# Placing the inverse exit of the second chunk pair by hand between the hidden-layer products of chunk 1

## The chip, the cores and the metric

The kernel runs on one core of a Trainium2 chip. The metric is device time in microseconds (us), from launch to end; the median of five runs of the kernel before is 590.45 us (586.62 to 592.89). Five engines work side by side, each through its own instructions in order: PE (TensorE, matrix products, with its weight loads shown as PEld), DVE (VectorE), ACT (ScalarE), POOL (GpSimd) and SP (SyncE, which only issues DMAs here). An instruction that waits for another engine holds up everything behind it on its own engine.

## The reference, cut to what matters

```python
# attention: delta rule, B=4, H=8, S=768, D=48
k_n = k / (norm(k) + 1e-6)
state = zeros(B, H, D, D)
for t in range(S):
    y[t]  = q[t] @ state                       # the state before this step's update
    v_old = state^T k_n[t]
    state = state + beta[t] * outer(k_n[t], v[t] - v_old)
# bridge (B,H,S,D) -> (B,S,384), then the MLP block
xn  = (x - mean(x)) / sqrt(var(x) + 1e-6) * g_ln
out = x + relu(xn @ w_ch1) @ w_ch2             # 384 -> 1536 -> 384
```

All of it is in float32.

## The kernel before, in words

The sequence is cut into 12 chunks of 64 tokens, and the 32 heads (batch times head) are laid out so that two batches share the 128 partitions. Within a chunk the recurrence is solved in closed form: the Gram matrix of the keys (`p_g`, line 358) is turned into the inverse of a unit triangular matrix (`xt`), and with it `recur` computes, in steps named KQ (products with the state, `p_k` and `p_y`, L640, then `v_raw` minus `p_k` on DVE, L645), U (L651), S (state update, L663 and L666), PU (L671), L1 and L2 (layer norm statistics) and N (transposes, L698). Chunks go in pairs.

**The inverse.** `inverse` works on DVE in a layout in which every partition holds one small block: a loop over columns, two instructions per column (L543, L548). For the first two pairs (`first_blocks`) the blocks are 16 by 16. The way out is `scatter`: two masked copies into `x_e` (L496) and a transpose into `own` (L499) for each chunk. From there `first_join` puts the 16-blocks together to blocks of 32: a transpose `x_n` (L593), 64 small matmuls `p_e` (L598), a copy with the sign changed on ACT (`es`, L601), 64 small matmuls `p_z` (L606) and an addition into `own` on DVE (L607). `to_xt` writes the blocks into `xt` (DVE L451 and ACT L453). `join` does the same once more, from 32 to 64, with `x_n` L559, `p_e` L568, `es` L581, `p_z` L614 and copies L619 on DVE and ACT. Its products for the second chunk of a pair are interleaved with the `p_z` of the first.

**The MLP.** `hidden` computes the 12 row blocks of the hidden layer of a chunk (`p_h`, L732, three matmuls each; `h` by ACT L736). Chunk 0 uses `ffn` (L749, sums on DVE L757); later chunks use `mlp`, with seven half-size products P1 to P7 (L787) and sums S1 to S4 and d1 to d7 on DVE (L792). It needs differences of blocks of the second weight matrix, made once (`sum_blocks`, L716, token T).

**What sets the order.** The first stretch (chunk 0 up to its layer norm) is written out in order. The second stretch is a `Plan`: generators are spread over a time axis by due times, and a scheduler orders the result; it holds chunk 1's recurrence, the hidden and output products of chunk 0, the weights and the preparation of chunks 2 and 3, among it the whole of the second pair's inverse and its joins. From chunk 2 on, each chunk is a slot whose order is a string of tokens, taken in exactly that order on every engine. The slots are not tied behind the plan, so the scheduler places the last instructions of the plan among the first of slot 2. In slot 2, H is one row block of chunk 1's hidden layer, KQ, U, S, PU, L1, L2 and N are steps of chunk 2's recurrence, T one block of `sum_blocks`, TK, TQ, G and PT prepare chunks 3 to 5, ga, sq and no begin the inverse of the next pair, Vk and Vs scale the next values by the key norms (`norms`, L402 to L410; `scale_v`, L418).

PSUM tiles are shared by tags: `p_o` of `ffn` and `p_h` take the same two buffers, and `p_e`, `p_z` and `p_n` take the same two.

Of the kernel before, what the change touches and what calls it, by code (L numbers as in the profile page):

```python
# [19 lines left out]
FB = 16  # L20
SLAB = 2
# [55 lines left out]
def in_turn(*gens):  # L77
    for gen in gens:
        yield from gen
# [3 lines left out]
def kernel(  # L83
# [23 lines left out]
    B, H, S, D = q.shape  # L107
    NCH = S // C
    NSL = NCH // SLAB
# [17 lines left out]
    def ps_att(shape, name):  # L127
        return psum.tile(shape, FP32, name=name, tag="att", bufs=2)
# [263 lines left out]
    def swapped(name):  # L392
        return blk.tile([128, 2 * FB * FB], FP32, name=name, tag="tr", bufs=2)

    def norm_parts(c, scratch=None):

        parts = [
            scratch[:, n::2, 0:D] if scratch is not None
            else swapped("ksq")[:, 0 : H * D].rearrange("p (h d) -> p h d", d=D)
            for n in range(2)  # L400
        ]
        nc.scalar.square(parts[0], k_of(c)[:, 0::2])  # L402
        for e in range(2):
            nc.scalar.square(parts[1][half(e)], k_of(c)[half(1 - e), 1::2])
        yield
        ksum = work.tile([128, GH], FP32, name="ksum")
        for n in range(2):
            nc.vector.tensor_reduce(out=ksum[:, n::2], in_=parts[n], axis=mybir.AxisListType.X, op=ALU.add)
        knrm = work.tile([128, GH], FP32, name="knrm")
        nc.scalar.sqrt(knrm, ksum)  # L410
        yield knrm

    def norms(c):
        *_, knrm = norm_parts(c)
        return knrm

    def scale_v(c, knrm):
        nc.vector.scalar_tensor_tensor(  # L418
            out=vs[c], in0=knrm[:, :, None].to_broadcast([128, GH, D]), scalar=1e-6, in1=vs[c],
            op0=ALU.add, op1=ALU.mult,  # L420
        )
# [7 lines left out]
    def prep_g(c, fine=False):  # L429

        new_chunk(c)
        turned(c, 0, True)
        yield
        for _ in gram(c, fine):
            pass
        yield

    def prep_p(c):

        turned(c, 1, True)  # L440
        yield
        yield from product(c)
        yield
# [4 lines left out]
    def to_xt(c, eng=None):  # L448

        xt, own = xts[c % NXT], halves.pop(c)  # L450
        nc.vector.tensor_scalar(out=xt[:, :, 0:BK], in0=own, scalar1=is_u[:, 0:1], scalar2=None, op0=ALU.mult)  # L451
        if eng is None:
            nc.scalar.copy(xt[:, :, BK:C], own)  # L453
        else:
            eng.tensor_copy(out=xt[:, :, BK:C], in_=own)
# [19 lines left out]
    def first_blocks(chunks):  # L475

        def gather(gb):
            for n, c in enumerate(chunks):
                tr = swapped("g_t").rearrange("p (s t) -> p s t", t=BK)
                nc.vector.transpose(  # L480
                    tr.rearrange("p s (b h) -> p s b h", b=2),
                    grams[c][:, :, 0:BK].rearrange("p h (b s) -> p s b h", b=2),
                )
                nc.vector.tensor_scalar(
                    out=gb[:, n], in0=tr[:, :, 0:FB], scalar1=is_b[:, 0:1], scalar2=None, op0=ALU.mult
                )
                nc.vector.scalar_tensor_tensor(
                    out=gb[:, n], in0=tr[:, :, FB:], scalar=is_b[:, 1:2], in1=gb[:, n], op0=ALU.mult, op1=ALU.add
                )

        def scatter(xb):
            own = blk.tile([128, len(chunks), GH, BK], FP32, name="own", tag="gb")
            for n, c in enumerate(chunks):
                xe = swapped("x_e").rearrange("p (b s t) -> p b s t", b=2, t=FB)
                for b in range(2):
                    nc.vector.tensor_scalar(  # L496
                        out=xe[:, b], in0=xb[:, n], scalar1=is_b[:, b : b + 1], scalar2=None, op0=ALU.mult
                    )
                nc.vector.transpose(  # L499
                    own[:, n].rearrange("p h (b t) -> p t b h", b=2), xe.rearrange("p b s t -> p t b s")  # L500
                )
                halves[c] = own[:, n]
                yield

        c0 = chunks[0]
        return inverse(len(chunks), FB, beta_f[:, c0 : c0 + len(chunks)], gather, scatter)
# [82 lines left out]
    def first_join(c):  # L589

        own, gsb = halves[c], grams[c]
        xn = swapped("x_n").rearrange("p (h t) -> p h t", t=BK)
        nc.vector.transpose(xn, own)  # L593
        quarters = [slice(BK * n, BK * n + BK) for n in range(4)]
        p_e = ps_att([128, GH, FB], "p_e")
        for h in range(GH):
            for q in quarters:
                nc.tensor.matmul(p_e[q, h], gsb[q, h, 0:BK], xn[q, h, 0:FB])  # L598
        es = work.tile([128, GH, BK], FP32, name="es", bufs=1)
        nc.gpsimd.memset(es[:, :, FB:], 0.0)  # L600
        nc.scalar.mul(es[:, :, 0:FB], p_e, -1.0)  # L601
        yield
        p_z = ps_att([128, GH, FB], "p_z")
        for h in range(GH):
            for q in quarters:
                nc.tensor.matmul(p_z[q, h], es[q, h], own[q, h, FB:])  # L606
        nc.vector.tensor_tensor(out=own[:, :, FB:], in0=own[:, :, FB:], in1=p_z, op=ALU.add)  # L607
        yield
# [326 lines left out]
    plan = Plan()  # L935
# [9 lines left out]
    plan.spread(ffn_0, FT // 2, 20, 42)  # L945
    plan.once(10, queries)
    plan.spread(in_turn(*(prep_g(c, True) for c in (2, 3))), 4, 16, 24)
    plan.spread(first_blocks((2, 3)), 5 + FB // 2, 24, 44)
    plan.spread(prep_p(2), 2, 30, 38)

    def then(c):
        yield from first_join(c)
        to_xt(c)
        yield

    plan.spread(in_turn(then(2), then(3)), 6, 44, 56)
    plan.once(50, lambda: scale_v(2, norms(2)))
    plan.spread(join((2, 3)), 4, 56, 62)
    with behind(tc, after):
        plan.run()  # L960

# [2 lines left out]


    orders = {
        2: """KQ H H H H H H T H T H T H T H U H H TK(a2) P1 S1 S2 d1 TK(b2) S P2 d2 S4 PU P6 d6
            S3 L1 G(a2) P5 d5 L2 TQ(b) P7 d7 N G(b2) P3 d3 ga PT(b) P4 d4 sq no Vk
            Vs""",
        3: """KQ H r H r H r H r U TQ(a2) H r H r H r S H r H r H H H PU P1 L1 S1 S2 d1 PT(a2) P2  # L970
            d2 L2 S4 P6 d6 S3 TK(a4) P5 d5 r N r P7 d7 G(a4) TK(b4) P3 d3 r G(b4) P4
            d4 r Vk Vs""",
# [13 lines left out]
    def slot(c, order):  # L986

        a = c - c % SLAB
        names = {"b": a + 1, "a2": a + 2, "b2": a + 3, "a4": a + 4, "b4": a + 5}
        begin(c)  # L990
        steps = mlp(c - 1)
        chunk = recur(c)
        if c + 2 < NCH:
            load_kv(c + 2)
        knrm = None
        for token in order.split():
            name, _, arg = token.partition("(")
            m = c // SLAB + (name[-1] != "'")
            name = name.rstrip("'")
            x = names[arg[:-1]] if arg else None  # L1000
            if name in steps:
                steps[name]()
            elif name in ("KQ", "U", "S", "PU", "L1", "L2", "N"):
                if not (name == "S" and c == NCH - 1):
                    next(chunk)
            elif name == "T":
                next(running_sums)
            elif name == "R":
                for _ in range(left.get(m, 0)):
                    next(inverses[m])  # L1010
                left[m] = 0
            elif name in ("ga", "sq", "no", "r", "own", "xt"):
                if m in inverses:
                    left[m] -= name == "r"
                    next(inverses[m])
            elif name in ("xn", "J"):
                if m in joins:
                    next(joins[m])
            elif name == "Vk":
                if c + 1 < NCH:  # L1020
                    knrm = norms(c + 1)
            elif name == "Vs":
                if c + 1 < NCH:
                    scale_v(c + 1, knrm)
            elif x < NCH:
                if name == "TK":
                    new_chunk(x)
                    turned(x, 0, True)
                elif name == "TQ":
                    turned(x, 1, True)  # L1030
                elif name == "G":
                    next(gram(x), None)
                elif name == "PT":
                    for _ in product(x):
                        pass

    running_sums = sum_blocks()
    inverses = {m: blocks(m) for m in range(2, NSL)}
    joins = {m: join((SLAB * m, SLAB * m + 1)) for m in inverses}
    left = {m: BK // 2 - 1 for m in inverses}  # L1040
    with in_this_order(tc):
        for c in range(SLAB, NCH):
# [34 lines left out]
```

## Time and profile before

| what | value |
| --- | --- |
| median of five runs | 590.45 us (586.62 to 592.89) |
| time of the profiled execution | 589.51 us |
| its span, first to last instruction | 587.4 us |
| mean granted TensorE clock | 0.948 |
| PE busy | 536.5 us (91%), 9938 matmul records |
| DVE busy | 384.3 us (65%) |
| ACT busy | 173.3 us (30%) |
| `p_h` L732 | 864 records, 202.5 us |
| `p_e`, `p_z` of the first joins, L598 and L606 | 512 records each, over four chunks |

A float32 matmul stands in the records twice, each with its own weight load; so one H is 6 records, one product of `first_join` is 128, of `join` 64, and KQ is 64 for `p_k` and 64 for `p_y`. The profile cuts the span into 40 slices and shows for each the busy share of every engine and the granted clock in tenths. In the timeline, "idle before" is time in which the engine did nothing, with what released it; "issue" there means that it waited for nothing that the profile shows.

### The profile page before, as it was taken

What the parts mean: (1) busy time and instruction counts of PE and PEld (TensorE: products, weight loads), DVE (VectorE), ACT (ScalarE), POOL (GpSimd) and SP (SyncE); (2) the same over time, 40 slices, a digit from 0 to 9 for tenths busy, and PEclk for the clock granted to TensorE, in tenths of its full rate; (3) what the DMA queues carried; (4) which work ended last, traced back from release to release, by engine and by line L of the source; (5) the groups of instructions that cost most, each with busy time, mean ns of one, the idle gap of its engine ahead of it and who ended that gap; (6) DMA issues with size and microseconds to landing.
All of it is one profiled execution on the core that took longest, in us unless ns stands there. A gap on an engine that the chain in (4) does not pass through costs nothing.

```text
span 587.4 us, 21790 instructions
## 1 busy us (share of the span) xinstructions
PE 536.5 (91%) x9938; PEld 459.2 (78%) x9938; DVE 384.3 (65%) x795; ACT 173.3 (30%) x355; POOL 16.3 (3%) x39
## 2 busy tenths in 40 slices
PE   5389886966999999999979999999999999999997
PEld 2165664655889898789878899888898898998997
DVE  5857978875236998489993889764899731522312
ACT  1233353111325215422216312336312142223120
POOL 5000200000000000000000000000000000000000
PEclk9568988885899999999999999999999999999999
DMA  4745979452123505222233313303303010010101
GB/s 57 142 156 115 216 173 204 74 89 41 20 26 59 88 7 83 57 30 50 42 48 61 63 19 66 45 4 68 46 8 77 2 30 2 2 29 1 28 0 28
DMA packets 158667, 34.57 MB, mean 59 GB/s; under 512 B 153952, under 2 KB 157040, under 8 KB 158576
## 3 DMA queue, kind: packets, MB, share of 16 engines
q1 hardware_dynamic: 144048, 22.28, 23.3%
q0 software_dynamic: 1456, 7.10, 3.8%
q10 hardware_dynamic: 13072, 3.80, 2.8%
q8 instruction: 78, 1.28, 0.9%
q14 instruction: 13, 0.11, 0.1%
HBM read 28.44 MB, written 4.72 MB: 56 GB/s over the span
## 4 chain that ended last, share of the span: by engine, by line
PE 70%; DVE 10%; issue 9%; ACT 3%; DMA 3%; SPq 1%; ACTq 1%; POOL 0%; DVEq 0%; POOLq 0%
PE p_h L732 30%; PE p_a L787 12%; PE p_o L787 9%; PE p_g L358 2%; DVE tmp L543 2%; DVE xb L548 2%; DMA words<-in_moe_w_ch_dram 2%; PE p_u L651 2%; PE p_e L568 2%; PE p_y L640 2%; PE p_y L671 2%; PE p_s L663 2%; PE p_k L640 2%; PE p_g L383 2%; PE p_z L614 2%
## 5 line engine op out<-in xcount | busy, mean ns | idle before, releaser
L732 PE MATMUL p_h<-xnt,w_sb 128*128 128x256 f32 x864 | 202.5, 390 | 0.7 <-ACT xnt L699 0.6
L732 PEld LDWEIGHTS p_h<-xnt,w_sb 128*128 128x128 f32 x864 | 163.8, 193 | 25.1 <-ACT xnt L699 0.9
L736 ACT ACTIVATE h<-p_h 128x256 f32<-128x256 f32 x144 | 55.2, 383 | 143.3 <-PE p_h L732 136.5
L548 DVE TENSOR_TENSOR xb<-xb,tmp 128x31 f32<-128x31 f32 (+20 forms) x154 | 50.1, 326 | 5.3
L787 PE MATMUL p_a<-t,h 128*128 128x192 f32 x264 | 47.1, 328 | 1.0 <-DVE h L792 1.0
L787 PE MATMUL p_o<-w_sb,h 128*128 128x192 f32 x264 | 48.0, 332 | 0.0
L543 DVE TENSOR_TENSOR tmp<-xb,gb 128x31 f32<-128x31 f32 (+15 forms) x124 | 42.0, 339 | 3.2
L787 PEld LDWEIGHTS p_a<-t,h 128*128 128x128 f32 x264 | 42.8, 190 | 1.5 <-DVE h L792 1.2
L787 PEld LDWEIGHTS p_o<-w_sb,h 128*128 128x128 f32 x264 | 42.7, 190 | 0.9
L682 DVE BATCH_NORM_STATS2 st<-x_ln 128x6 f32<-128x384 f32 x24 | 12.9, 542 | 34.9 <-ACT x_ln L676 34.8
L830 PE MATMUL p_w<-zeros 128*64 128x512 f32 (+1 forms) x30 | 20.1, 809 | 14.0 <-DVE zeros L827 10.8
L619 DVE COPY xt<-p_z 32x512 f32<-32x512 f32 x12 | 8.1, 679 | 29.6 <-PE p_z L614 29.6
L792 DVE TENSOR_TENSOR s<-h 128x768 f32<-128x768 f32 x11 | 10.2, 931 | 26.4 <-ACT h L736 26.4
L787 PE MATMUL p_a<-t,s 128*128 128x192 f32 x132 | 23.6, 329 | 2.9 <-DVE o L792 2.8
L699 ACT COPY xnt<-p_n 128x384 f32<-128x384 f32 x24 | 10.3, 482 | 48.9 <-PE p_n L698 48.8
L787 PEld LDWEIGHTS p_a<-t,s 128*128 128x128 f32 x132 | 21.5, 190 | 3.9 <-DVE o L792 3.7
L787 PE MATMUL p_a<-w_sb,h 128*128 128x192 f32 x132 | 24.2, 333 | 0.0
L787 PE MATMUL p_o<-w_sb,s 128*128 128x192 f32 x132 | 23.6, 328 | 0.0
L358 PEld LDWEIGHTS p_g<-kt 48*32 48x32 f32 (+1 forms) x1024 | 14.1, 125 | 11.4 <-issue 8.3
L358 PE MATMUL p_g<-kt 48*64 48x64 f32 (+2 forms) x1024 | 16.0, 225 | 6.8 <-issue 5.3
L830 PEld LDWEIGHTS p_w<-zeros 128*64 128x64 f32 x30 | 4.8, 184 | 21.8 <-DVE zeros L827 10.9
L787 PEld LDWEIGHTS p_a<-w_sb,h 128*128 128x128 f32 x132 | 21.3, 190 | 0.6
(123 smaller groups left out, 728.8 us busy)
## 6 DMA issues: line engine op xcount, KB each, us to landing
words<-in_moe_w_ch_dram POOLq DMA_DIRECT2D x9, 768.0 KB, 5.8
out_dram<-o SPq DMA_DIRECT2D x48, 96.0 KB, 3.3
k<-in_k_dram SPq DMA_DIRECT2D x44, 96.0 KB, 2.8
v_raw<-in_v_dram SPq DMA_DIRECT2D x22, 192.0 KB, 4.1
tb<-in_k_dram SPq DMA_DIRECT2D x48, 64.0 KB, 2.8
tb<-in_q_dram SPq DMA_DIRECT2D x44, 64.0 KB
words<-in_moe_w_ch_dram ACTq DMA_DIRECT2D x3, 768.0 KB
tb<-in_q_dram SPq DMA_DIRECT2D x44, 32.0 KB, 2.2
```

Of the source, the lines that this page charges most:

```text
L358: nc.tensor.matmul(out_, kt[rows, i, r0 : r0 + (BK if fine else C)], kt[rows, i, r0:C])
L383: nc.tensor.matmul(p_g[half(e ^ hp), hp, j], kt[rows, i], qt[rows, i])
L543: nc.vector.tensor_tensor(out=t, in0=xb[:, :, 0:n, j : j + 1].to_broadcast([128, nb, n, w]), in1=gb[:, :, j : j + 1, j + 1 : L].to_broadca ...
L548: nc.vector.tensor_tensor(out=rest, in0=rest, in1=t, op=ALU.subtract)
L568: nc.tensor.matmul(p_e[r1, h], gsb[r0, h, BK:C], xn[r0, h])
L614: nc.tensor.matmul(p_z[r0, h], es[r1, h], xt[r1, h, BK:C])
L640: nc.tensor.matmul(dst[half(e), hp, j], kq[n][rows, e * GP + j], s_all[rows, e, j], start=(n == 0 or j == 0), stop=(n == 0), skip_group_ch ...
L682: nc.vector.bn_stats(out=st[:, g], in_=y[:, g])
L732: nc.tensor.matmul(p_h, w1_sb[:, t, f * 128 : (f + 1) * 128], xnt[:, t], start=(t == 0), stop=(t == KC - 1),)
L736: nc.scalar.activation(h[f // HF][:, f % HF], p_h, ACTF.Relu)
L787: nc.tensor.matmul(p[n], a[:, f], b[:, f], start=(first and f == 0), stop=(f == HF - 1), skip_group_check=True,)
L830: nc.tensor.matmul(p_w[0:64, 0:width], zeros, zeros[:, None, :].to_broadcast([128, width, 64]), start=True, stop=True,)
```

## The change

The steps that bring the second pair (chunks 2 and 3) out of the block layout leave the plan and become tokens in slot 2. The column loop stays in the plan; its spread ends at due time 42 in place of 44 and is not run to its end. X is one step of `scatter` (one chunk), F one half of `first_join`, W `to_xt`, J' one step of `join` of this pair. The squares, sums and scaling for chunk 2's values (`norms` and `scale_v`) move from due time 50 to 28. Within slot 2, S and PU now stand ahead of P1, and U, T, TK(a2), TK(b2), L1, L2 and N have other places. No arithmetic is added or left out.

```diff
-    plan.spread(first_blocks((2, 3)), 5 + FB // 2, 24, 44)
+    inv_1 = first_blocks((2, 3))
+    plan.spread(inv_1, 2 + FB // 2, 24, 42, whole=False)
     plan.spread(prep_p(2), 2, 30, 38)
-    def then(c):
-        yield from first_join(c)
-        to_xt(c)
-        yield
-    plan.spread(in_turn(then(2), then(3)), 6, 44, 56)
-    plan.once(50, lambda: scale_v(2, norms(2)))
-    plan.spread(join((2, 3)), 4, 56, 62)
+    plan.once(28, lambda: scale_v(2, norms(2)))
...
-        2: """KQ H H H H H H T H T H T H T H U H H TK(a2) P1 S1 S2 d1 TK(b2) S P2 d2 S4 PU P6 d6
-            S3 L1 G(a2) P5 d5 L2 TQ(b) P7 d7 N G(b2) P3 d3 ga PT(b) P4 d4 sq no Vk
-            Vs""",
+        2: """H H X F(a) H X F(a) F(b) W(a) H KQ F(b) W(b) J' H J' T H T H J' T H U J' T H H S H H
+            PU P1 L1 S1 S2 d1 TK(a2) P2 d2 L2 S4 TK(b2) P6 d6 S3 G(a2) P5 d5 N TQ(b) P7 d7
+            G(b2) P3 d3 ga PT(b) P4 d4 sq no Vk Vs""",
...
+            elif name == "X":
+                next(inv_1)
+            elif name == "F":
+                next(first_joins[x])
+            elif name == "W":
+                to_xt(x)
...
-    joins = {m: join((SLAB * m, SLAB * m + 1)) for m in inverses}
+    joins = {m: join((SLAB * m, SLAB * m + 1)) for m in range(1, NSL)}
+    first_joins = {c: first_join(c) for c in (2, 3)}
```

## The prediction

> **What bounds the kernel now.** I read the page's slices first.
>
> ```profile
> PE   5389886966999999999979999999999999999997
> ...
> PEclk9568988885899999999999999999999999999999
> ```
>
> PE is full from the eleventh slice (147 us) on, but for one later dip, and the clock is at nine tenths or more from the twelfth. The change lies in slices 9 and 10 (117 to 147 us), with PE digits of 6 and clock digits of 8 and 5: there PE is a third idle and, for most of it, at half clock. The PE timeline from the end of chunk 0's output products (121.6 us) shows why:
>
> ```profile
> 121.59 1.15 PE L640 MATMUL p_k<-s_all,kt 48*64 48x48 f32 x64
> 122.56 0.30 PE L640 MATMUL p_y<-s_all,qt 48*64 48x48 f32 x8
> 125.80 1.60 PE L598 MATMUL p_e<-x_n,gsb 32*32 32x16 f32 x128 [2.95 <-DVE x_n L593]
> 127.33 1.10 PE L640 MATMUL p_y<-s_all,qt 48*64 48x48 f32 x30
> 128.79 0.40 PE L606 MATMUL p_z<-own,es 32*32 32x16 f32 x14 [0.36 <-ACT es L601]
> 130.34 1.72 PE L606 MATMUL p_z<-own,es 32*32 32x16 f32 x113 [1.14 <-issue]
> ...
> 134.62 1.78 PE L598 MATMUL p_e<-x_n,gsb 32*32 32x16 f32 x114 [2.38 <-issue]
> 136.33 0.67 PE L640 MATMUL p_y<-s_all,qt 48*64 48x48 f32 x14
> 138.07 0.45 PE L640 MATMUL p_y<-s_all,qt 48*64 48x48 f32 x4 [1.07 <-issue]
> ...
> 142.17 0.29 PE L606 MATMUL p_z<-own,es 32*32 32x16 f32 x5 [1.83 <-issue]
> ...
> 145.79 5.73 PE L732 MATMUL p_h<-xnt,w_sb 128*128 128x256 f32 x14
> ```
>
> Two things. First, four waits of 1.07 to 2.38 us whose releaser is "issue", and between them always 128 records: 113 and the 15 that follow, 114+14, 4+124. 128 records with their weight loads are 256 instructions, and the page's instruction queue moved 78 packets, 1.28 MB, 16 KB each. I read these as waits for code: a block starts 4.28, 3.45 and 4.10 us after the one before it, when small matmuls eat 128 records in under 2 us. I take **4.0 us a block**. Second, the granted clock, in windows between its changes:
>
> ```profile
> 123.46:126.87 3.41, 1.07 (x111) 1.08 (x112) 3.18 (x6) 0.15 (x1) 0.00 (x0) 1.00 0.74 112
> 126.87:130.29 3.42, 1.95 (x68) 1.60 (x60) 1.95 (x4) 1.90 (x5) 0.00 (x0) 0.50 0.32 74
> ...
> 143.94:147.35 3.41, 3.41 (x69) 3.08 (x69) 3.41 (x5) 1.18 (x2) 0.00 (x0) 0.50 0.00 0
> 147.35:150.77 3.42, 3.42 (x10) 2.70 (x9) 0.38 (x1) 0.69 (x2) 0.00 (x0) 0.50 0.00 0
> 150.77:154.18 3.41, 3.41 (x140) 2.58 (x138) 0.68 (x1) 1.35 (x4) 0.00 (x0) 1.00 0.02 5
> ```
>
> (PE busy is the second figure, the clock the third from the end.) One window with a third of PE work takes the clock to 0.50. A window full of work of which half is small joins does not bring it back; the next, only `p_h`, does.
>
> **The change, step by step.** Prices at full and half clock: H 1.3 us (38 records in 8.47) and 2.45 (14 in 5.73); a first-join product 1.2 (128 in 1.25 at 61 us) and 1.95 (114 in 1.78); a join product 1.1 (64 in 1.13 at 241.9) and 1.85 (64 in 1.92 at 143.9); KQ 2.1 (1.15+1.11 at 189.8) and about 4.3 (30 `p_y` records in 1.10, less the overlap of the last, 34 ns each, times 128); U, S, PU 1.1 and, unseen at half clock, 1.1 to 2.2 by KQ's ratio, of which I take 2.1. I lay the new order on the old clock:
>
> - DVE ends the columns at 122.0. The two sums of `norms` (0.55 each, once at 127.3 and 129.2) now stand among the columns: 123.1. Their ACT squares fall into ACT's 16 us of idle time before 126.7, at no cost; were the keys late (their DMAs are issued at 100, medians 2.8 us), each us would delay the columns by one. One `x_e` (0.3) and the two sums that free the PSUM buffers (0.98 for both) let the first H start at **124.1**. PE has nothing else, as KQ now stands behind: 2.5 us lost.
> - H H to 126.7. DVE: `x_e`, `own` 1.05, `x_n` 0.70 give 126.6, so F(a) follows at once, to 127.9. Code blocks: before, 116 records lie between the last output product and a block's start (64+8+44). After, these are 12 of H H and 104 of `p_e`: a block starts at 127.7, the next is due at 131.7.
> - H to 129.2 hides `es` (0.36). `p_z` has 98 records in this block, to 130.1, **waits for code until 131.7**, ends 132.0.
> - DVE's addition L607 stands ahead of chunk 3's `x_n`: 0.42+0.70 and handovers, 133.3. F(b): 98 records to 134.2, code at 135.7, end 136.2. Between 129.2 and 136.2 PE sees no H: room for a whole window with little work, so **the clock falls**, as at 126.87.
> - At half clock: H to 138.6, KQ to 142.9 (92 records, then the block due at 139.7, long there; next due 145.7), `p_z` 92 records to 144.3, code 145.7, end 146.2, H to 148.7 (covers the addition, L451 and `x_n` on DVE, 1.6), `p_e` of the join to 150.6, H H to 155.4. In these 4.9 us of pure `p_h` the clock comes back, say at 154: 155.0.
> - Full clock: interleaved joins 1.3 (128 records, 151.45 to 152.74 before) to 156.3, H to 157.6 while L619 copies `xt` (0.68+0.58). U's code block is due at 159.1: end 160.2. `p_z` 161.3, H H with one code wait of 1.0 to 164.9, S 166.0, H H 168.6, PU 169.7, P1 and P2 (2.0+2.1) 173.8. P6 waits for d1, whose engine DVE must first do L1 (after ACT's 0.8: 1.45), S1, S2 (1.9), d1 (0.35): **174.4**.
>
> Before, the same products end at 174.26, where P6 starts. From there both orders hold the same work, and PE or the DVE work of slot 3 simply shifts. DMAs: SP's queue keeps its order; the waits it has on DVE's transposes (loads for chunks 4 and 5) move by the 1 us or so that slot 2 does. The T blocks (4 of 1.3 on DVE) stay in DVE's idle time (6.79 and 5.15 us before), and POOL's `es` clear (0.3) lies under the addition.
>
> Sum: 174.4 - 174.3 = +0.1. The six waits of the timeline above (9.7 us from 2.95 to 1.83) are gone, but 2.5 us before the first H, code waits of 1.6, 1.5, 1.4, 1.2 and 1.0, and H and KQ at half clock (2.2 for KQ, 1.15 for each H) stand in their place. The clock's windows are not tied to the program; a return one window later costs up to 1.7 us, half of it on average: +0.9. On the profiled execution's 589.5 us (its span 587.4 and 2.1 around it; 0.9 under the median): **590.5 us**.
>
> **Two rules weighed.** The trace's window 143.94 to 147.35 is busy throughout and leaves the clock at 0.50. The Trainium skill (TensorE: Matmul & The Clock Gate, "What's actually happening") gives the clock back after one busy window of about 3.4 us; H and KQ would then return it near 140.5, and a second fall would follow in the next code wait: about 589. The trace's waits of 1.07 to 2.38 us fall on every 128 records. The skill (Runtime: NRT & Kernel Launch, "Instruction fetch mechanics") has the same 256-instruction blocks, but calls crossing one mostly hidden; without the five new ones (6.7 us) the sum would be 583.8.
>
> **Rivals.**
> - *The clock holds* (15%). H before and after each small product keeps it up: the windows at 58.6 to 75 us, with first-join products of chunk 1 among H, stay at 1.00. Against it: 7 us without H. H at 136.0 to 137.3, KQ 140.3 with a code wait of 0.9, `p_z` 144.1, H 145.4, joins and H's 152.3, U 154.7, PU 164.2: 5.5 us less, **585**.
> - *The clock holds and code is hidden* (8%): H's slow appetite lets the blocks arrive. The waits above sum to about 8.7 us, half of them only cover DVE's `own`-`x_n` chain: **580.5**.
> - *The clock stays down past H H* (27%), the slower side. It returns only after a window of nothing but H; 4.9 us of H H hold such a window for fewer than half of the phases ((4.9-3.4)/3.4). If not, single H's between joins come, and the joins (+0.9), H (+1.15), U (+1.0, partly in its code wait), `p_z` (+0.75) and H H (+2.3) run at half clock: +3, and with S, H H and PU +7.5. **595.5**. It decides at the window after 150 us.
> - *The change does not reach the end* (5%): the DVE-bound slots 3 to 5 (DVE busy 9.2 to 9.8 of 10 us from 255 to 305) swallow a shift: 590.
>
> My forecast has 45%. From these cases: faster by over 1% (below 584; 1% is about what a measurement of this kernel can tell) 0.14, the second rival and part of the first; slower by over 1% (above 595) 0.20, the upper part of the third and U's bounds; within 0.66. The range, 582 to 598, leaves out the code-hidden case and the longest stay at half clock.
>
> **What would show it.** After: the first `p_h` of slot 2 near 124.1 with DVE's L757 as releaser; "issue" waits again every 128 records, the first inside chunk 2's `p_z`; clock 0.50 from about 134 to 154; P6 near 174.4. Wrong if the clock stays at 1.00 through 136 to 150, if a block takes clearly less than 3.5 us, or if a new wait stands before U or P6.

## The result

The changed kernel takes 589.33 us (median of 43 runs, 585.0 to 599.78), the kernel before 591.97 us beside it (80 runs, 586.62 to 597.41): a ratio of **0.9962, 95% interval 0.9948 to 0.9975**. It is faster by 2.3 us, where 0.1 to 1 us slower had been forecast. A later set of runs gave 0.9991 (0.9962 to 1.0020), so the gain is between nothing and half a per cent. Ratios leave out runs over 1.5% above the fastest run of their kernel, while medians take in all runs, so a ratio need not be the quotient of the medians beside it.

The first profile of it doesn't show that gain at all: its span is 591.6 us, 4.2 us more than that of the kernel before. The slices say where it went. PE and granted clock, changed kernel:

```profile
PE   5379886978999999899978999999999999999997
...
PEclk9578996995899999889999899999999999999999
```

The weak place is still the tenth and eleventh slice (133 to 163 us). But there are new clock digits of 8 at slices 17, 18 and 23, around 248 to 255 and 326 to 330 us, in slots that the change doesn't touch. The PE timeline of the changed kernel, from the first H of slot 2 on (start, us, operation, records, idle before):

```profile
123.45 2.83 PE L732 MATMUL p_h<-xnt,w_sb 128*128 128x256 f32 x12 [2.21 <-DVE o L757]
126.21 1.43 PE L598 MATMUL p_e<-x_n,gsb 32*32 32x16 f32 x128
127.57 1.56 PE L732 MATMUL p_h<-xnt,w_sb 128*128 128x256 f32 x6
129.06 0.99 PE L606 MATMUL p_z<-own,es 32*32 32x16 f32 x97
130.53 0.44 PE L606 MATMUL p_z<-own,es 32*32 32x16 f32 x31 [0.47 <-issue]
132.22 1.48 PE L598 MATMUL p_e<-x_n,gsb 32*32 32x16 f32 x97 [1.26 <-DVE x_n L593]
136.08 0.62 PE L598 MATMUL p_e<-x_n,gsb 32*32 32x16 f32 x31 [2.38 <-issue]
136.63 2.93 PE L732 MATMUL p_h<-xnt,w_sb 128*128 128x256 f32 x6
139.49 1.96 PE L640 MATMUL p_k<-s_all,kt 48*64 48x48 f32 x64
141.23 1.92 PE L640 MATMUL p_y<-s_all,qt 48*64 48x48 f32 x64
143.09 2.21 PE L606 MATMUL p_z<-own,es 32*32 32x16 f32 x128
145.22 2.93 PE L732 MATMUL p_h<-xnt,w_sb 128*128 128x256 f32 x6
148.08 1.52 PE L568 MATMUL p_e<-x_n,gsb 32*32 32x32 f32 x64
149.53 2.86 PE L732 MATMUL p_h<-xnt,w_sb 128*128 128x256 f32 x12
```

Up to 132 us this is the forecast order of events: the first H behind DVE's L757, F(a) at once behind H H, a code wait inside the first `p_z`, another inside the second chunk's `p_e`. Then it departs from it. The code wait in the second `p_z` is missing, and H H at 149.53 runs at full speed (12 records in 2.86 us), where half clock until about 154 had been forecast. The stretch from the end of chunk 0's last output product to KQ of slot 3 is 66.0 us (121.25 to 187.23); before it was 67.3 us (121.66 to 188.98). So the part of the kernel that changed did become shorter, by 1.3 us in this profile, and the later clock periods gave more than that back: KQ of slot 7 starts 4.2 us later than before.

### The profile page after: what moved, and what is told of

It is laid out like the page before. It is cut to its first block, busy times and chain, and to the rows that moved or that the text cites. A ratio compares the mean times of both kernels' runs of the same rounds, so it can differ in the third digit from the quotient of the medians.

```text
span 591.6 us, 21793 instructions
## 1 busy us (share of the span) xinstructions
PE 542.1 (92%) x9938; PEld 461.2 (78%) x9938; DVE 384.7 (65%) x795; ACT 173.2 (29%) x355; POOL 16.9 (3%) x39
## 4 chain that ended last, share of the span: by engine, by line
PE 69%; DVE 11%; issue 9%; DMA 4%; ACT 3%; ACTq 1%; SPq 1%; POOL 0%; DVEq 0%; POOLq 0%
PE p_h L732 30%; PE p_a L787 12%; PE p_o L787 8%; PE p_g L358 2%; DVE tmp L543 2%; DVE xb L548 2%; DMA words<-in_moe_w_ch_dram 2%; PE p_k L640 2%; PE p_u L651 2%; PE p_y L640 2%; PE p_z L614 2%; PE p_e L568 2%; PE p_y L671 2%; PE p_g L383 2%; PE p_s L663 1%
## 5 line engine op out<-in xcount | busy, mean ns | idle before, releaser
L732 PE MATMUL p_h<-xnt,w_sb 128*128 128x256 f32 x864 | 206.2, 395 | 2.9 <-DVE o L757 2.2
L548 DVE TENSOR_TENSOR xb<-xb,tmp 128x31 f32<-128x31 f32 (+20 forms) x154 | 50.1, 326 | 5.3
L787 PE MATMUL p_a<-t,h 128*128 128x192 f32 x264 | 47.1, 328 | 1.0 <-DVE h L792 1.0
L787 PE MATMUL p_o<-w_sb,h 128*128 128x192 f32 x264 | 47.9, 331 | 0.0
L787 PEld LDWEIGHTS p_a<-t,h 128*128 128x128 f32 x264 | 42.7, 190 | 1.5 <-DVE h L792 1.2
L787 PEld LDWEIGHTS p_o<-w_sb,h 128*128 128x128 f32 x264 | 42.8, 190 | 0.8
L682 DVE BATCH_NORM_STATS2 st<-x_ln 128x6 f32<-128x384 f32 x24 | 13.0, 544 | 38.6 <-ACT x_ln L676 38.5
L830 PE MATMUL p_w<-zeros 128*64 128x512 f32 (+1 forms) x30 | 21.6, 862 | 14.0 <-DVE zeros L827 10.8
L787 PE MATMUL p_a<-t,s 128*128 128x192 f32 x132 | 23.7, 329 | 3.2 <-DVE o L792 3.2
L787 PEld LDWEIGHTS p_a<-t,s 128*128 128x128 f32 x132 | 21.5, 190 | 4.4 <-DVE o L792 4.4
L787 PE MATMUL p_a<-w_sb,h 128*128 128x192 f32 x132 | 24.3, 334 | 0.0
L787 PE MATMUL p_o<-w_sb,s 128*128 128x192 f32 x132 | 23.6, 328 | 0.0
L358 PEld LDWEIGHTS p_g<-kt 48*32 48x32 f32 (+1 forms) x1024 | 14.4, 126 | 10.7 <-issue 6.9
L830 PEld LDWEIGHTS p_w<-zeros 128*64 128x64 f32 x30 | 4.8, 187 | 22.4 <-DVE zeros L827 10.9
L787 PEld LDWEIGHTS p_o<-w_sb,s 128*128 128x128 f32 x132 | 21.6, 190 | 0.2
L787 PEld LDWEIGHTS p_a<-w_sb,h 128*128 128x128 f32 x132 | 21.2, 190 | 0.6
```

The costliest lines, as they stand in the source:

```text
L358: nc.tensor.matmul(out_, kt[rows, i, r0 : r0 + (BK if fine else C)], kt[rows, i, r0:C])
L548: nc.vector.tensor_tensor(out=rest, in0=rest, in1=t, op=ALU.subtract)
L682: nc.vector.bn_stats(out=st[:, g], in_=y[:, g])
L732: nc.tensor.matmul(p_h, w1_sb[:, t, f * 128 : (f + 1) * 128], xnt[:, t], start=(t == 0), stop=(t == KC - 1),)
L787: nc.tensor.matmul(p[n], a[:, f], b[:, f], start=(first and f == 0), stop=(f == HF - 1), skip_group_check=True,)
L830: nc.tensor.matmul(p_w[0:64, 0:width], zeros, zeros[:, None, :].to_broadcast([128, width, 64]), start=True, stop=True,)
```

## The experiments

A short name for what recurs: the *stretch* is the time from the end of the last `p_o` of chunk 0 to the first `p_k` of slot 3, in one profile.

### The order of the tail alone

The tail of slot 2 (S, PU and L1 around P1) goes back to the old order, all else as changed.

```diff
-  ... T H U J' T H H S H H PU P1 L1 S1 S2 d1 TK(a2) P2 d2 L2 S4 TK(b2) P6 d6 S3 G(a2) P5 d5 N TQ(b) P7 d7
+  ... T H U J' T H H H H TK(a2) P1 S1 S2 d1 TK(b2) S P2 d2 S4 PU P6 d6 S3 L1 G(a2) P5 d5 L2 TQ(b) P7 d7 N
```

> The changed kernel with the steps after the twelfth hidden block in the old order (P1 S1 S2 d1, then S and PU among the products). Theory A, the gain comes from the waits that H, F and J fill between 121 and 160 us: nothing is lost, ratio to the kernel before 0.994 to 0.998, and P6 no longer waits for d1 (0.4 us in the changed kernel's profile). Rival B, the gain comes from moving S and PU ahead of P1: ratio back at 0.999 to 1.002.

Measured: 589.34 us, ratio 0.9967 (0.9932 to 1.0003), about the changed kernel's. The interval still reaches into rival B's range, so the ratio alone doesn't exclude it. But the stretch is 64.5 us, among the changed kernel's 64.0 to 66.0 in its three profiles, so the new order behind the joins isn't needed for the shorter stretch; and P6 no longer waits for d1, as expected.

### The norms alone

The kernel before, with only `norms` and `scale_v` moved from due time 50 to 28.

```diff
-    plan.once(50, lambda: scale_v(2, norms(2)))
+    plan.once(28, lambda: scale_v(2, norms(2)))
```

> The kernel before with one edit: the squares, sums and scaling of chunk 2's values at due time 28 in place of 50. Theory A: ACT's es of chunk 2 (128.29 us before, behind a square) and chunk 3's x_n come up to 1 us earlier, but the columns end 1.1 us later, so ratio 0.998 to 1.002. Rival C, this move alone is what the change gains: 0.995 to 0.997.

Measured: 589.39 us, ratio 0.999 (0.9961 to 1.0019). Stretch 67.7 us, clock at 0.50 for 27.3 us of it. In the stretch it behaves as the kernel before: what is gained there comes with the joins between the H products.

### One H more in the gap

An H stands between the first chunk's `p_z` and the second chunk's `p_e`, where the changed kernel waits longest; it is taken from behind the second J', where the changed kernel has two.

```diff
-  H H X F(a) H X F(a) F(b) W(a) H KQ F(b) W(b) J' H J' T H T H J' ...
+  H H X F(a) H X F(a) H F(b) W(a) H KQ F(b) W(b) J' H J' T H T J' ...
```

> The changed kernel with one H moved from between the two join steps to between chunk 2's p_z and chunk 3's p_e, where PE waited 1.26 us for DVE's x_n and 2.38 us for code in the changed kernel's profile. Theory A (PE's idle time there is on the path): 1.3 us less than the changed kernel, ratio to the kernel before 0.992 to 0.995; if the granted clock also stays at 1.00 through 131 to 149 us, 0.986 to 0.990. Rival D (the code block's arrival sets the end of chunk 3's p_e, whatever stands before it): same as the changed kernel, 0.996.

Measured: 589.12 us, ratio 0.9979 (0.9944 to 1.0014). The gap was filled (its code wait fell from 2.38 to 0.66 us, the wait for `x_n` went), and the clock, down from 131.55 to 134.97, was up again before KQ. But a code wait of 2.12 us then stood in the second `p_z`, the clock fell there (145.20 to 152.03), and the time is not clearly different. Here the wait that was filled turned up at the next block.

### KQ first

KQ goes back to the head of the slot, where the kernel before has it; its DVE subtraction stays where KQ was (`recur` yields once more for this chunk). In the first kernel H is spread anew as well, in the second only KQ moves.

```diff
+            if c == SLAB: yield          # between KQ's products and its subtraction
-  H H X F(a) H X F(a) F(b) W(a) H KQ F(b) W(b) J' ...
+  KQ H H X F(a) H X F(a) H F(b) W(a) KQ H F(b) W(b) J' ...      # first kernel
+  KQ H H X F(a) H X F(a) F(b) W(a) H KQ F(b) W(b) J' ...        # second kernel
```

> The changed kernel with KQ's products back at the head of slot 2, where PE idled 2.2 us, their subtraction on DVE left where it was, and one H each between F(a) and F(b) and behind F(b). Theory A: KQ at full clock in idle time and gone from the stretch at half clock (3.6 us there), so 3 to 4 us less than the changed kernel, ratio to the kernel before 0.988 to 0.991; 0.984 if the clock holds. Rival D (code blocks set the pace of the stretch): KQ's 128 records are one block wherever they stand, so under 1 us less, 0.995.

> The changed kernel with KQ's products at the head of slot 2 and every H where the change has it (its subtraction stays where KQ was). Theory A: this alone holds most of the gain of the version with KQ first and H spread anew: ratio to the kernel before 0.990 to 0.993. Rival I, the H between F(a) and F(b) does it by keeping the clock up: 0.995 or more here.

Measured: 583.51 us, ratio 0.9902 (0.9862 to 0.9941), and 584.78 us, ratio 0.991 (0.9877 to 0.9944). Stretches 59.6 and 60.4 us, 3.6 to 6.4 us under the changed kernel's. The timeline of the second kernel:

```profile
119.47 1.15 PE L640 MATMUL p_k<-s_all,kt 48*64 48x48 f32 x64
120.44 1.11 PE L640 MATMUL p_y<-s_all,qt 48*64 48x48 f32 x64
121.65 2.83 PE L732 MATMUL p_h<-xnt,w_sb 128*128 128x256 f32 x12
...
134.89 0.62 PE L598 MATMUL p_e<-x_n,gsb 32*32 32x16 f32 x31 [3.42 <-issue]
135.44 2.93 PE L732 MATMUL p_h<-xnt,w_sb 128*128 128x256 f32 x6
138.30 1.91 PE L606 MATMUL p_z<-own,es 32*32 32x16 f32 x128
```

KQ fills the 2.2 us in which the changed kernel's first H waits for DVE's output sums, at full clock (2.1 us; 3.6 in the changed kernel's first profile), and it no longer lies between H products at half clock. In the first kernel KQ takes 2.0 us at the head as well, but the first H still waits 1.90 us behind it for those sums. The gain of the second held although the code wait in the second `p_e` grew from 2.38 to 3.42 us.

### The changed kernel again, twice

Nothing is edited.

> The changed kernel itself once more, for a second profile. Theory E (the windows of the clock gate are not tied to the program, and falls outside the change, as at 247.89 and 326.40 us in the first profile, come and go between executions): the first products of slot 2 start within 1 us of where they did, counted from the last output product, but the falls after 200 us lie elsewhere or are missing, and the span differs by 2 to 7 us from 591.6. Rival F (the change itself causes the two falls): they are there again, at 244 to 255 and 326 to 330 us. Ratio to the kernel before 0.995 to 0.998 in both.

> The changed kernel a third time, for a third profile. Theory K: the clock is down in the stretch for 7 to 21 us (20.5 and 10.2 us in its first two profiles), less than in the kernel before profiled beside it, and the stretch from the last output product to slot 3's KQ is 63.5 to 66.5 us (66.0 and 64.6 us before). If it is down for 24 us or more, the profiles of the two kernels don't differ in clock as the means over the runs do.

Measured: 589.5 us, ratio 0.9991 (0.9962 to 1.0020), and 585.73 us in one run. The spans of the two profiles are 582.5 and 583.6 us, against 591.6 us of the first: **one kernel, 9 us apart**. The ratio is a little above the 0.995 to 0.998 that was expected. Of the 9.1 us between the first profile and the shortest, 6.6 lie behind the start of slot 3, where the clock is down for 10.2 us in the first and never in the shortest; the third profile has two falls of 3.4 us there, at 242.3 and 296.9 us. So rival F, falls made by the change itself at 244 to 255 and 326 to 330 us, doesn't hold. The stretches are 64.5 and 64.0 us, the clock is down in them for 10.2 and 17.1 us (20.5 in the first). In the first of the two profiles here the code block inside the second `p_z` is late, as forecast, but KQ is at full speed:

```profile
135.78 0.62 PE L598 MATMUL p_e<-x_n,gsb 32*32 32x16 f32 x31 [1.83 <-issue]
136.33 2.93 PE L732 MATMUL p_h<-xnt,w_sb 128*128 128x256 f32 x6
139.19 1.15 PE L640 MATMUL p_k<-s_all,kt 48*64 48x48 f32 x64
140.15 1.11 PE L640 MATMUL p_y<-s_all,qt 48*64 48x48 f32 x64
141.20 0.94 PE L606 MATMUL p_z<-own,es 32*32 32x16 f32 x90
143.65 0.50 PE L606 MATMUL p_z<-own,es 32*32 32x16 f32 x38 [1.51 <-issue]
```

With KQ at half clock no wait follows (first and third profile: 3.6 us each); with KQ at full clock one does (2.1 and 1.51 us). In these profiles the two are alternatives, and the forecast had charged both.

### The kernel before again

> The kernel before once more, for a second profile of its stretch from the last output product to slot 3's KQ. Theory K (the change's gain is clock): the joins, p_y and little else fill that stretch, so the clock is down there for 20 us or more again (23.9 us in its first profile, 27.3 us with only the norms changed), and the stretch is 66.5 to 69 us. If the clock is down for only 7 to 14 us, as in five of the profiles with the joins between the H products, theory K falls.

Measured: 592.78 us in one run, span 590.6 us. Stretch 66.8 us, clock down for 23.9 us of it, the very figure of the first profile. This is what was expected if the clock is the gain, though less waiting would shorten the stretch as well ("What the gain is" below looks at both). Both kernels vary, but in the stretch the kernel before (three profiles with that of the norms: 66.8 to 67.7 us, 23.9 to 27.3 us of half clock) and the changed one (three profiles: 64.0 to 66.0 us, 10.2 to 20.5 us) don't overlap.

### Are the "issue" waits code?

32 small products of zeros, whose result is used by nothing, are put far ahead (at some 13 us), which shifts every later TensorE instruction by 64 instructions of the stream.

```diff
+        p_w = ps_ffn([128, 8, 64], "p_w")
+        for _ in range(32):
+            nc.tensor.matmul(p_w[0:64, 0, 0:8], zeros, zeros[:, 0:8], start=True, stop=True)
```

> The changed kernel with 32 tiny products (64 records) of a tile of zeros added at about 13 us, in PE's idle time, results unused. Theory G (an issue wait comes where a code block of 128 records begins): the waits move by 64 records, from the 98th record of chunk 2's p_z and of chunk 3's p_e to the 34th of each, and from the last record of chunk 3's second join product into the product of U. Rival H (the waits belong to the instruction, say to a matmul after a semaphore): they stay at the 98th. Time: 0.5 to 2 us either way, ratio to the kernel before 0.994 to 0.999.

Measured: 588.24 us, ratio 0.9947 (0.9918 to 0.9975). The span of its profile is 593.4 us, far over the median, so only the places of the waits are read from it:

```profile
132.26 0.98 PE L606 MATMUL p_z<-own,es 32*32 32x16 f32 x94 [1.15 <-issue]
...
136.37 1.48 PE L598 MATMUL p_e<-x_n,gsb 32*32 32x16 f32 x95 [1.26 <-issue]
...
144.55 1.57 PE L606 MATMUL p_z<-own,es 32*32 32x16 f32 x101 [1.28 <-issue]
```

The waits moved from behind record 97 to behind 34 in the first `p_z` and from 97 to 33 in the second `p_e`, by the 64 records that the added products have; in the second `p_z` one stands behind record 27, where the changed kernel's second profile has it behind 90. The third place that was expected, inside U, shows no wait. They belong to places in the instruction stream, one every 128 records, and not to the products' data: rival H doesn't hold.

That it is code they wait for can be read from the DMA packets that the traces hold. In the 14 profiles of this study PE has 50 waits by "issue" between 110 and 170 us, and each ends 1.2 to 1.8 us after a packet of 16384 bytes on the instruction queue (q8) has ended.

### Work in the gap, to hold the clock

Three 64x512 products of zeros (2.79 us, result used by nothing) between the first chunk's `p_z` and the second chunk's `p_e`.

```diff
-  H H X F(a) H X F(a) F(b) W(a) H KQ ...
+  H H X F(a) H X F(a) WARM F(b) W(a) H KQ ...
+            elif name == "WARM":
+                keep_warm(3)
```

> The changed kernel with three 64x512 products of zeros put on TensorE between the first pair of p_z and the second chunk's p_e, where it stands for 1.26 us on x_n and then 2.38 us for code in the changed kernel's first profile; their result is used by nothing. Over the runs so far the mean granted clock was 0.944 (54 runs of the kernel before), 0.944 (11 runs with only the norms changed) and 0.950 (51 runs of the changed kernel), and within one kernel a run is 2.7 to 4.3 us shorter for every 0.01 of mean clock. Theory K: what the change gained is clock alone, and idle TensorE in this gap is what still loses it. Then the fall of the clock near 132 goes, H and KQ run in 1.6 and 2.1 us, the mean granted clock is 0.953 or above, and the ratio to the kernel before is 0.990 to 0.994. Theory L: the wait for the code block, not the clock, sets the stretch; 2.6 us of added work lies beside a wait that ends when the block is there, the time stays within 0.3 per cent of the changed kernel (0.994 to 0.999), whatever the clock does. Theory M: the block is counted from the moment TensorE's sequencer gets past the x_n wait, so the added products push p_e by 1 to 1.3 us and the block with it: 0.998 to 1.002.

Measured: 590.65 us, ratio 0.998 (0.9942 to 1.0017); stretch 63.3 us. Theory K fails as a recipe: the clock didn't stay up, it fell at 137.5 instead of 132 us, behind the code wait, and KQ ran at half clock (3.6 us). The ratio lies in theory L's range and at the edge of M's, and its interval covers both. Counted from the last output product, the second part of `p_e` started 15.9 us in, against 14.8, 15.5 and 15.0 in the changed kernel's three profiles; but the code packet that it waited for started 3.3 us after the block before it began, against 3.1, 2.6 and 3.4, so M's delay of the block by 1 to 1.3 us is not seen. The stretch is shorter than in each of those three profiles without a better ratio, which stays open.

### KQ first, and the sums out of the way

The first KQ kernel, with the norms' sums and scaling on DVE moved back behind the columns (VK, VS); then the same with the two output sums of chunk 0's MLP ahead of the last columns (O).

```diff
-  KQ H H X F(a) H X F(a) H F(b) W(a) KQ H ...
+  KQ H H X F(a) H X VK F(a) H F(b) W(a) VS KQ H ...       # first kernel
+  KQ O H H X F(a) H X VK F(a) H F(b) W(a) VS KQ H ...     # second kernel
+            if f % 2: yield              # in ffn, so that O is a step of its own
```

> The version with KQ first and H spread anew, and the move of the values' norms undone: the squares stay early on ACT, but the two sums on DVE wait until chunk 3's own is out and the scaling until chunk 3's x_n is. Theory A (the columns' end sets the first H and the first x_n): these start up to 1.1 us earlier, ratio to the kernel before 0.985 to 0.989. Rival J (the scheduler then puts both PSUM sums behind own again, and the first H waits for them): no gain over the version it is made from, 0.989 to 0.992.

> The run with KQ at the head and the norms' sums late, changed in one thing: the two output sums of the first MLP (the DVE instructions that the first H waits for) stand ahead of the last five DVE instructions of the pair's columns, instead of behind own. There the first H waited 2.26 us behind KQ for them. Theory P (path): H H begins some 1.5 to 2.0 us earlier, x_n comes no later since the sums stood ahead of it already, and the ratio to the kernel before falls from 0.986 to 0.981 to 0.984. Theory C (code): H H's end moves up but the next wait for a code block takes 1 us or more of it (0.93 us to 2 us in that run's p_e of the second chunk), and the ratio stays at 0.984 to 0.988.

Measured: 582.40 us, ratio **0.9859** (0.9822 to 0.9895), and 582.42 us, ratio **0.9845** (0.9801 to 0.9890). Both beat both kernels. The first has theory A's ratio, but not its mechanism: its first H starts 4.3 us behind the last output product, against 3.9 in the kernel that it is made from, because it waits 2.26 us for the output sums as rival J had it; its profiled stretch is 61.2 us against 59.6. Why its time is better is open. In the second, H H follows KQ at once, 1.9 us behind the last output product instead of 4.3; the next three code waits are 1.23, 1.48 and 0.27 us (1.17, 0.93 and 1.15 us in the first). The ratio lies at the lower end of theory C's range, just outside P's, and its interval covers both, so the run doesn't tell them apart. The path is 2.3 us shorter at its head and the stretch is 3.1 us shorter (58.1 us); the ratios differ by 0.0014, or 0.8 us, with intervals so wide that neither 0 nor 2.3 us is excluded.

## Why the prediction was wrong

**The milestones.** Time from the end of chunk 0's last output product, as the prediction's steps had it and in the three profiles of the changed kernel, in us:

| milestone | predicted | first | second | third |
| --- | --- | --- | --- | --- |
| first H starts | 2.5 | 2.2 | 2.1 | 2.1 |
| KQ starts | 17.0 | 18.2 | 18.9 | 18.4 |
| H H behind the join's `p_e` starts | 29.0 | 28.3 | 26.8 | 28.3 |
| that H H ends | 33.4 | 31.1 | 29.6 | 31.2 |
| U ends | 38.6 | 34.9 | 33.4 | 35.0 |
| P6 starts | 52.8 | 51.2 | 49.7 | 49.3 |

In the two profiles of the kernel before P6 starts at 52.6 and 52.1 us. The mean of the three is 50.1: the change takes 2.3 us off, and the steps had it at +0.1. That the forecast of 590.5 us lies 1.2 us from the measured median is partly luck: the kernel before ran at 591.97 us beside it, not at 590.45, and errors of both signs stand in the steps. From KQ's start to the start of H H they are 1.9 to 4.1 us too long, in H H 1.5, from there to U's end 1.4; but KQ starts 1.2 to 1.9 us later than they say, and from U's end to P6 they are 2.1 us too short in two of the three profiles.

**Right.** The head: the first H behind L757 (at +2.1 to 2.2 us, forecast +2.5), F(a) straight behind H H, the loss of cover when KQ moved away. The code waits as such, their unit of 128 records, and the first two places. The clock's fall in the gap before the second `p_e` (132 us, forecast between 129 and 136). The wait before P6 (0.39 to 0.40 us, a new one): the steps have it (173.8 to 174.4), although the list of signs calls a new wait before P6 a sign of being wrong. That nothing changes behind P6: from P6 to slot 3's KQ it is 14.7 us in both kernels. That DMAs don't matter: no wait of PE in the stretch is put down to one. The norms' move alone is within noise (0.999).

**The step that failed: "At half clock: H to 138.6, KQ to 142.9 ... H H to 155.4. In these 4.9 us of pure `p_h` the clock comes back, say at 154".** From KQ's start to H H's end it allotted 16.4 us; measured were 12.9, 10.7 and 12.8. H H ran at full clock in all three (2.9 us where the steps have 4.4), because the clock was back at 148.9, 139.2 and 146.7 us and not at 154. The half-clock windows of the changed kernel, first all of PE (busy time is the second figure, the clock the third from the end), then `p_h` alone in the same windows:

```profile
138.66:142.07 3.41, 3.41 (x99) 2.76 (x101) 0.55 (x1) 0.38 (x1) 0.00 (x0) 0.50 0.00 0
142.07:145.49 3.42, 3.39 (x172) 3.15 (x166) 0.55 (x2) 0.00 (x0) 0.00 (x0) 0.50 0.02 5
145.49:148.90 3.41, 3.41 (x36) 2.40 (x38) 3.34 (x6) 1.00 (x2) 0.00 (x0) 0.50 0.02 5
148.90:152.31 3.41, 3.41 (x54) 2.79 (x49) 1.23 (x1) 1.56 (x3) 0.00 (x0) 1.00 0.02 5
```

```profile
138.66:142.07 3.41, 0.90 (x3) 0.18 (x1) 0.38 (x1) 0.50 0.00 0
142.07:145.49 3.42, 0.27 (x1) 0.27 (x2) 0.00 (x0) 0.50 0.02 5
145.49:148.90 3.41, 2.66 (x6) 1.58 (x6) 0.38 (x1) 0.50 0.02 5
```

Three windows in which PE is busy throughout. The two that are mostly filled by KQ and `p_z` leave the clock at 0.50; the third, with 2.66 us of `p_h`, returns it. In the second profile the window before KQ was enough:

```profile
135.79:139.21 3.42, 2.88 (x6) 1.85 (x6) 0.00 (x0) 0.50 0.02 5
139.21:142.62 3.41, 0.04 (x1) 0.00 (x0) 0.38 (x1) 1.00 0.02 5
```

The prediction had taken from the kernel before that a window must hold almost nothing but `p_h`. There the window that didn't return the clock had less than half:

```profile
143.94:147.35 3.41, 1.63 (x5) 1.29 (x5) 0.00 (x0) 0.50 0.00 0
147.35:150.77 3.42, 3.42 (x10) 2.70 (x9) 0.69 (x2) 0.50 0.00 0
```

Between 1.63 and 3.42 that trace says nothing, and the prediction chose the upper end. Worked out from the records of all 14 profiles of this study: every half-clock window after 110 us with 2.09 us or more of products that use all 128 rows (`p_h`, L749, L787, L698, L830) was the last of its period, none with under 1.38 was, and in between both occur. This is what the records show together, and no run varied it by itself. A single H at half clock has 2.93 us; so one H at the right phase is enough, where the steps demanded two behind each other.

Two prices in the step were off too. KQ at half clock took 3.6 us, not 4.3. H took 2.93, not 2.45: the 14 records in 5.73 us, from which the price came, end at 151.52, and from 150.77 on they ran at full clock.

What the sum left out is a second fall, which only the weighed rule had. It came in the first profile (159.14 to 162.55) and the second (156.27 to 159.69), not in the third. In the first two the H H behind U ran at half clock (12 records in 4.54 us, from 158.50 in the first); in the third they took 2.86 us.

**The second term: code.** The steps let a block come every 4.0 us and charged waits of 1.6, 1.5, 1.4, 1.2 and 1.0 us, 6.7 in all. Measured: 0.47, 2.38, none, none and 0.93 in the first profile (3.8), 1.60, 1.83, 1.51 and 0.93 in the second (5.9), and 0.41, 2.66 and 0.60 in the third (3.7). (For the fourth, in U, the steps themselves have about 1.4: H ends at 157.6 and the block is due at 159.1.) The block inside the second `p_e` starts 5.0 to 5.8 us after the one before it (130.53 to 136.08 in the first profile), and the ones behind H products are there in time. Its packet is late: it starts 3.1, 2.6 and 3.4 us after the block before it began, where in the kernel before the next packet starts 1.0 to 1.7 us after the blocks of its four waits began. Only 31 records of the block before it come ahead of the gap between the two products. With an H or the products of zeros in the gap in place of the wait for `x_n` the packet is as late (2.6 to 3.5 us); in the kernel with 32 products ahead, where 94 records stand between the block's start and the same wait, it starts after 1.7 us. So the delay goes with what stands behind those 31 records, and not with the wait for `x_n` as such; what in the hardware asks for the packet is not shown.

**What the gain is.** Each run has a mean granted clock. Over the runs that were compared:

| kernel | runs | mean granted clock | ratio |
| --- | --- | --- | --- |
| before | 71 | 0.9432 | 1 |
| norms alone | 11 | 0.9436 | 0.999 |
| changed | 51 | 0.9496 | 0.9962, 0.9991 |
| tail as before | 9 | 0.9499 | 0.9967 |
| H in the gap | 10 | 0.9500 | 0.9979 |
| 32 products ahead | 10 | 0.9501 | 0.9947 |
| zeros in the gap | 8 | 0.9511 | 0.998 |
| KQ first, H spread | 6 | 0.9530 | 0.9902 |
| KQ first only | 9 | 0.9510 | 0.991 |
| KQ first, norms late | 6 | 0.9575 | 0.9859 |
| the same, output sums early | 6 | 0.9525 | 0.9845 |

A straight-line fit over the 158 runs of the later sets, with a level for each chip and each kernel, gives 3.6 us less (standard error 0.3) for 0.01 more of clock. By this slope the changed kernel's 0.0064 would be 2.3 us, as much as it gained in the first set. At equal clock the fit, which holds only the 12 runs of its second set, has it 1.0 us (0.55) *behind* the kernel before, and the KQ-first kernels 2.4 to 4.7 us ahead of it. The fit is an association: no run set the clock by itself, and the one that tried (zeros in the gap) only moved the fall.

The profiles divide the gain differently. In the stretch PE is idle for 10.1 and 9.5 us and busy for 57.2 and 57.3 in the two profiles of the kernel before; in the three of the changed one it is idle for 7.9, 10.1 and 7.6 and busy for 58.1, 54.3 and 56.4. Of the mean difference of 2.2 us, 1.3 are less waiting and 0.9 less time for the same products, of which less runs at half clock (17.1 and 18.1 us busy there before; 17.7, 8.3 and 14.0 after). These means hide a wide spread between profiles, so how much of the gain is clock and how much is filled waits stays open; by the profiles it is some of each.

**The rivals.** "The clock holds" (585) had the sign, but the clock fell in all profiles. "The clock stays down past H H" (595.5) got the larger chance because of the same misreading. The hidden code (580.5) is excluded by the waits of 0.4 to 2.7 us in the changed kernel's profiles. Of the two rules that were weighed, the first (the Trainium skill, TensorE: Matmul & The Clock Gate, "What's actually happening": one busy window returns the clock) would have given "about 589", which is where the median lies, with a second fall as it said; but the full windows at 138.66 and 142.07 above stayed at 0.50, so as it stands it holds here only for windows of large products. The other (Runtime: NRT & Kernel Launch, "Instruction fetch mechanics": crossing a block mostly hidden) does not agree with these runs where small products eat a block in 1.5 to 2 us: the waits there are 0.4 to 3.4 us.

## What to carry to other kernels

Where a stage of small products runs at half clock, look in the windows between the clock's changes for how much of each is large products, and bound the clock's return from both sides before choosing; here the choice of one end put 1.5 us into H H alone, where the whole sum was +0.1. Where a half-clock product stands ahead of a wait for code, ask whether it hides the wait before charging both. And cover that is taken away at one place (KQ from the slot's head) may be worth more than what the same instructions gain at the new one: putting KQ back, with or without spreading H anew, was worth 0.5 to 0.9% on top of the change, across sets of runs.

## What the runs showed that was not expected

The same program's span differs by 9 us between profiles (582.5 and 591.6) with equal instructions. Most of it goes with half-clock periods of 3.4 to 6.8 us in stages that the change doesn't touch (around 245, 300 and 325 us); they come and go between executions, and the second profile of the kernel before has them too (247.5, 302.1 and 322.6 us). A single profile of this kernel can therefore have the opposite sign of the comparison, as the first one here did.
